# Two transformer layers on one core: the mean of a layernorm as one GpSimd operation per ScalarE tile, and a re-searched instruction order

## The chip, the cores and the metric

One core of a Trainium2 chip. The metric is the device time of the whole program in microseconds (us), the median of several runs. Engines: PE (TensorE matmul, with PEld, its weight loads), DVE (VectorE), ACT (ScalarE), POOL (GpSimd), SP (SyncE, which here issues DMAs).

## The reference

x has 2048 rows of 512 in bfloat16. Four steps run one after the other, each with a residual: A, B, A, B, with the same weights in both layers.

```
x = x + _A_ref(_layernorm(x), A_wqkv, A_w_phi, A_wo)
x = x + _B_ref(_layernorm(x), B_W_gate, B_W_up, B_W_down)
...
phi_q = concat([softmax(q @ w_phi), softmax(-q @ w_phi)]);  phi_k likewise     # 32 heads of 16
kv = phi_k^T v;  z = sum(phi_k);  o = (phi_q kv) / (phi_q z + 1e-6);  A = o @ wo
h = gate * (gate > 0) * up;  B = h @ W_down                                    # F = 1376
```

The attention is linear: kv is one small matrix per head, summed over all 2048 rows. No query can be finished before the last key has been added to kv.

## The kernel before

The rows are 16 tiles of 128 (t = 0 to 15), four to a chunk (c = 0 to 3). A recording layer, `Plan`, notes every operation with its engine; a table of numbers, `ORDER`, then says in which order the operations are written out, and since each engine works its own list in order, that table is the whole schedule. The planner's costs (`TINY`, `X_IN`, the second argument of `pl.op`) steer only the search that once made the table: at build time they have no effect. `BEHIND`, a list of waits that would keep VectorE and GpSimd apart on the port they share, is empty in both kernels.

For each layer and tile:

- **Norm** (class `Norm`). VectorE takes `bn_stats` (line 364) and `bn_aggr` (366); GpSimd adds eps (372) and takes the power -0.5 (374). Tiles are grouped (one or two). A tile is then normalised by the engine that its letter in `STEP["xn1"]` (layer 0) or `STEP["xA"]` (layer 1) names: A is ScalarE (436), D is VectorE and P is GpSimd (448). ScalarE computes scale*x + bias and needs -mean*rstd as its bias; GpSimd makes it in two operations per group, -mean (422) and the product with rstd (424). In layer 1 the chunks c < `STEP["sA"]` take another way (`add_sums`): the residual add on VectorE also gives the sum (542, with an accumulator read), ScalarE gives the sum of squares (388), and six small GpSimd operations follow.
- **Turn**: the normalised tile is transposed, by PE and a copy out of PSUM (457, 259) in the first chunks, by a DMA that SP issues (462, 466) in the others.
- **Keys and values** (`keys_values`): matmul (686), two exponentials on ScalarE (707), values (639, 257), sums over features on VectorE (658, 664, 668; a half may be pre-added by GpSimd, 655), reciprocal (716), and the scale of the features (721), cut between GpSimd and VectorE by a digit of `STEP["ks0"]`. Then PE adds the tile to kv (744): the sums.
- **Queries** (`queries`): matmul (786), exponentials (790), sums, a reciprocal (795), a small product (799, VectorE or GpSimd by `STEP["qq0"]`), a scale (806, by `STEP["qs0"]`), a DMA transpose (808). Queries of the last chunk are held until all sums are done.
- **Attention** (`attention`): after kv is masked into R (766), PE multiplies queries by R (825), VectorE divides (843, 845), the result is turned and projected (876) and added to x (542). Only one PSUM tile of kind q serves 825, so one tile's division must be read out before the next.
- **GLU** (`glu`): gate and up matmuls (589, 569), ScalarE copies (595, 599), VectorE products (602, 606), down (621), residual add (546).

In the names of rows, `sk`, `rk` are the sums and reciprocals of keys, `sq`, `rq` those of queries, `bnst`, `mv` the statistics, `b` any working tile, `ps` and `q` PSUM. Groups of the plan are called k0.5 (keys, layer 0, tile 5), f0.1 (query features), a0.0 (attention) and so on below.

Of the kernel before, what the change touches and what calls it, by code (L numbers as in the profile page):

```python
# [8 lines left out]
P = 128  # L9
# [16 lines left out]
Alu = mybir.AluOpType  # L26
# [3 lines left out]
F32 = mybir.dt.float32  # L30
# [98 lines left out]
WF_IN, WK_IN, WV_IN, WQ_IN, LOADED = 3.57, 5.83, 10.1, 14.03, 13.0  # L129
X_IN = [3.35, 4.26] + [6.46] * 2 + [8.61] * 4 + [11.37] * 4 + [12.62] * 4  # L130
TINY = 0.165
# [197 lines left out]
class Norm:  # L329
# [82 lines left out]
    def normalise(self, n, mv, rstd):  # L412
        st, nc, pl = self.st, self.st.nc, self.st.pl
        tiles, self.tiles, self.mv = self.tiles, [], None
        self.groups.pop(0)
        engs = [self.eng[t % len(self.eng)] for t in tiles]
        nmr = None
        if "A" in engs or self.sums:
            nmr = Buf("ve", [P, 4], F32)
            if not self.sums:  # L420
                self.neg = u = Buf("u", [P, 4], F32)
                pl.op("POOL", TINY, lambda: nc.gpsimd.tensor_scalar_mul(out=u[:, 0:n], in0=mv[:, 0:n, 0], scalar1=-1.0),
                      reads=[(mv, j) for j in range(n)], writes=[(u, 0)])
            pl.op("POOL", TINY, lambda u=self.neg: nc.gpsimd.tensor_tensor(out=nmr[:, 0:n], in0=u[:, 0:n], in1=rstd[:, 0:n], op=Alu.mult),
                  reads=[(self.neg, 0), (rstd, 0)], writes=[(nmr, 0)])
        joint = n == 2 and self.pairs[tiles[0] // 2] == "2" and not any(self.turn and self.turn[t % TPC] != "-" for t in tiles)
        both = Buf("b2", [P, 2, D], BF16) if joint else None
        for j, t in enumerate(tiles):
            ti = t % TPC
            xn = None if joint else Buf("b1", [P, D], BF16)  # L430
            key = (both, j) if joint else (xn, 0)
# [3 lines left out]
            if engs[j] == "A":  # L435
                pl.op("ACT", 0.705, lambda to=to, t=t, j=j: nc.scalar.activation(
                    out=to(), in_=st.X[:, t, :], func=AF.Identity, scale=rstd[:, j:j + 1], bias=nmr[:, j:j + 1]),
                    reads=[("X", t), (rstd, 0), (nmr, 0)], writes=[key])
            else:
# [3 lines left out]
                def scalars(j=j, nmr=nmr):  # L443
# [7 lines left out]
                    reads=[("X", t), (rstd, 0)] + ([(nmr, 0)] if self.sums else [(mv, q) for q in range(n)]), writes=[key], port=not by_pool, long=by_pool)  # L451
# [361 lines left out]
def attention(st, c, pT, norm, L):  # L813
# [72 lines left out]
    "tB0": "A---", "tB1": "---A", "tA": "----", "wev": "ADADAAAADDDAAAAA", "xn1": "APAPDAADPAAPAAAA",  # L886
    "st": "DDDDDDDDDDDDDDDD", "turn": "AAADDAAD", "wake": 20, "fuse0": "AFAA", "fuse1": "FFFF", "gate": 3, "sA": 3,
# [6 lines left out]
}  # L894
ORDER = [int(i) for i in """
# [157 lines left out]
```

## Time and profile before

| | us |
|---|---|
| median of 3 runs (376.4 to 376.66) | 376.47 |
| the profiled execution's own time | 376.54 |
| its span, first to last instruction | 374.8 |
| PE busy | 367.1 |
| DVE busy | 264.1 |
| ACT busy | 210.4 |
| POOL busy | 139.4 |

The granted TensorE clock is 1.00 in every stretch of 10 us. The profile page gives busy shares, the chain of work that ended last, and the costliest groups. A PE that is called busy may be waiting inside a pipelined matmul, but here 512-column matmuls start every 0.215 to 0.216 us over most of the span.

### The profile page before, as it was taken

How to read it: one execution, taken by the hardware profiler on the slowest of the kernel's cores; microseconds unless marked ns; L12 is line 12 of the kernel's file. 1: busy time of each engine (PE TensorE's matmuls, PEld its weight loads, DVE VectorE, ACT ScalarE, POOL GpSimd, SP SyncE). 2: the span in 40 equal slices, each digit the busy share in tenths (PEclk: the TensorE clock that was granted, in tenths of full speed). 3: DMA queues.
4: the chain of work that ended last, by engine and by line, in shares of the span. 5: the costliest groups of instructions: out<-in, count | busy, mean ns of one | idle time of the engine just before them, and what ended most of it. 6: DMA issues, size and time to landing. Idle time of an engine off the chain costs nothing.

```text
span 374.8 us, 6931 instructions
## 1 busy us (share of the span) xinstructions
PE 367.1 (98%) x2530; PEld 195.8 (52%) x2530; DVE 264.1 (70%) x606; ACT 210.4 (56%) x478; POOL 139.4 (37%) x226
## 2 busy tenths in 40 slices
PE   7999989999999999999999999999999999999996
PEld 3454545877645454444444446575546444444453
DVE  6999999997789964486556796898947551244432
ACT  5999987868856525874485184875433334121200
POOL 6999989363140306063522457235200100100000
PEclk9999999999999999999999999999999999999999
DMA  8692694878844407300033045157653501200121
GB/s 259 181 224 46 172 240 90 122 114 156 111 80 91 85 0 115 70 0 2 11 47 71 14 59 100 39 116 127 127 101 71 86 0 31 70 0 16 28 64 63
DMA packets 95746, 31.83 MB, mean 85 GB/s; under 512 B 87424, under 2 KB 95200, under 8 KB 95712
## 3 DMA queue, kind: packets, MB, share of 16 engines
q1 hardware_dynamic: 93024, 27.97, 38.9%
q10 hardware_dynamic: 2688, 3.42, 2.7%
q8 instruction: 20, 0.33, 0.4%
q14 instruction: 14, 0.11, 0.1%
HBM read 8.44 MB, written 2.10 MB: 28 GB/s over the span
## 4 chain that ended last, share of the span: by engine, by line
PE 83%; DVE 8%; POOL 6%; DMA 1%; issue 1%; ACTq 0%
PE ps L589 37%; PE ps L621 20%; PE ps L876 7%; PE ps L786 4%; PE ps L686 4%; PE ps L639 4%; PE ps L569 3%; PE q L825 2%; DVE bnst L364 2%; POOL b L721 1%; PE q L744 1%; DMA X<-in_A_x_dram 1%; DVE b L721 1%; POOL b L655 1%; POOL b L448 1%; DVE rk L716 1%
## 5 line engine op out<-in xcount | busy, mean ns | idle before, releaser
L599 ACT ACTIVATE b<-ps 128x512 bf16<-128x512 f32 (+3 forms) x110 | 50.2, 482 | 61.8 <-PE ps L589 61.1
L589 PE MATMUL ps<-b,wu 128*128 128x512 bf16 (+3 forms) x440 | 81.6, 321 | 0.0
L589 PE MATMUL ps<-b,wg 128*128 128x512 bf16 (+3 forms) x440 | 81.4, 321 | 0.0
L621 PE MATMUL ps<-wd,b 128*128 128x512 bf16 (+4 forms) x374 | 78.7, 366 | 0.0
L621 PEld LDWEIGHTS <-b 128*128 128x128 bf16 (+1 forms) x374 | 35.5, 98 | 39.8
L589 PEld LDWEIGHTS <-wg 128*128 128x128 bf16 x440 | 38.9, 98 | 32.4
L589 PEld LDWEIGHTS <-wu 128*128 128x128 bf16 x440 | 38.5, 98 | 30.0
L602 DVE SCALAR_TENSOR_TENSOR b<-ps,b 128x512 bf16<-128x512 f32 (+2 forms) x60 | 34.1, 594 | 22.0 <-ACT b L599 11.3
L721 POOL TENSOR_TENSOR b<-b,rk 128x1024 bf16<-128x1024 bf16 (+6 forms) x27 | 38.2, 1427 | 24.1 <-DVE rk L716 15.3
L790 ACT ACTIVATE b<-ps 128x512 bf16<-128x512 f32 x64 | 35.8, 618 | 14.3 <-PE ps L786 12.3
L707 ACT ACTIVATE b<-ps 128x512 bf16<-128x512 f32 x64 | 36.4, 637 | 4.2 <-PE ps L686 3.9
L655 POOL TENSOR_TENSOR b<-b 128x256 f32<-128x256 bf16 x39 | 26.7, 701 | 30.8 <-ACT b L790 12.3
L686 PE MATMUL ps<-Wk,b 128*128 128x512 bf16 x128 | 32.4, 379 | 0.0
L876 PE MATMUL ps<-wo,b 128*128 128x512 bf16 x128 | 32.2, 379 | 0.0
L786 PE MATMUL ps<-Wq,b 128*128 128x512 bf16 x128 | 32.2, 379 | 0.0
L639 PE MATMUL ps<-wkv,b 128*128 128x512 bf16 x128 | 31.8, 379 | 0.3 <-ACT b L707 0.3
L546 DVE SCALAR_TENSOR_TENSOR X<-ps,r,X 128x512 bf16<-128x512 f32 (+2 forms) x22 | 14.9, 694 | 22.3 <-PE ps L621 22.3
L542 DVE SCALAR_TENSOR_TENSOR X<-ps,X 128x512 bf16<-128x512 f32 x32 | 21.8, 682 | 8.8 <-PE ps L876 8.4
L595 ACT ACTIVATE b<-ps 128x128 bf16<-128x128 f32 (+2 forms) x50 | 20.8, 431 | 6.5 <-PE ps L589 5.5
L806 POOL TENSOR_TENSOR b<-b,rq 128x512 bf16<-128x512 bf16 x23 | 23.9, 1048 | 0.5
L524 ACT ACTIVATE sq<-b 128x512 bf16<-128x512 bf16 x32 | 20.2, 632 | 6.2 <-DVE b L503 6.0
L845 DVE TENSOR_TENSOR b<-q,dd 128x512 bf16<-128x512 f32 x32 | 21.8, 683 | 0.6
(94 smaller groups left out, 477.1 us busy)
## 6 DMA issues: line engine op xcount, KB each, us to landing
out_dram<-X SPq DMA_DIRECT2D x15, 128.0 KB, 1.9
X<-in_A_x_dram ACTq DMA_DIRECT2D x3, 512.0 KB, 6.4
b<-b SPq DMA_TRANSPOSE x91, 3.1
wd<-in_B_W_down_dram SPq DMA_DIRECT2D x5, 256.0 KB, 3.2
wg<-in_B_W_gate_dram SPq DMA_DIRECT2D x8, 160.0 KB, 3.1
wu<-in_B_W_up_dram SPq DMA_DIRECT2D x8, 160.0 KB, 3.2
wkv<-in_A_wqkv_dram ACTq DMA_DIRECT2D x2, 512.0 KB, 5.6
wq<-in_A_wqkv_dram ACTq DMA_DIRECT2D x1, 512.0 KB, 3.9
```

The source lines that it names most:

```text
L589: nc.tensor.matmul(ps[:], lhsT=wt[:, b, f * P:(f + 1) * P], rhs=xnT[:, lo:hi, b, :], start=(b == 0), stop=(b == NDB - 1))
L599: pl.op("ACT", 0.045 + 0.43 * share, lambda ups=ups, ru=ru, sign=1.0 if fuse else -1.0: nc.scalar.activation(out=ru[:], in_=ups[:], func=A ...
L602: pl.op("DVE", 0.058 + 0.548 * share, dur=0.138 + 0.548 * share, fn=lambda gps=gps, ru=ru, h=h, cs=cs: nc.vector.scalar_tensor_tensor(out= ...
L621: nc.tensor.matmul(yps[:], lhsT=hs[f][:fsz, ti * P:(ti + 1) * P], rhs=st.wd[:fsz, f, cols], start=(f == 0), stop=(f == NFT - 1))
L639: nc.tensor.matmul(vp[:], lhsT=xnT[:, ti, kb, :], rhs=st.wkv[:, kb, D:2 * D], start=(kb == 0), stop=(kb == NDB - 1))
L655: nc.gpsimd.tensor_tensor(out=h[:].rearrange("p j h f -> p j f h"), in0=x[:, :, 0], in1=x[:, :, 1], op=Alu.add)
L686: nc.tensor.matmul(ps[:], lhsT=xnT[:, ti, kb, :], rhs=w(kb), start=(kb == 0), stop=(kb == NDB - 1))
L707: pl.op("ACT", 0.48, lambda s=s, ek=ek, pk=pk: nc.scalar.activation(out=ek[:, :, s, :], in_=pk[:].rearrange("p (j x) -> p j x", j=8), func ...
L721: eng.tensor_tensor(out=phiK[:, lo:hi, :, :].rearrange("p j s (f h) -> p (j s) f h", h=4), in0=ek[:, lo:hi, :, :].rearrange("p j s (f h) - ...
L786: nc.tensor.matmul(pq[:], lhsT=xnT[:, ti, kb, :], rhs=st.Wq2[:, kb, :], start=(kb == 0), stop=(kb == NDB - 1))
L790: pl.op("ACT", 0.48, lambda s=s, eq=eq, pq=pq: nc.scalar.activation(out=eq[:, :, s, :], in_=pq[:].rearrange("p (j x) -> p j x", j=8), func ...
L876: nc.tensor.matmul(yps[:], lhsT=turned(b), rhs=st.wo[:, b, :], start=(b == 0), stop=(b == NDB - 1))
```

## The change

- The bias of a ScalarE tile, -mean*rstd, becomes one GpSimd `tensor_scalar` (mean times rstd times -1, on 128x1) for each tile whose letter is A. The two operations per group (422, 424) go. Where sums are used the old form stays, but `sA` falls from 3 to 0, so that no chunk uses sums: all 12 tiles concerned in layer 1 take `bn_stats` and `bn_aggr` on VectorE, and the ScalarE squares go.
- `xn1`: tiles 3 and 8 are normalised by VectorE, no longer by GpSimd (P to D); tiles 1 and 11 stay with GpSimd.
- `qs0`, `qq0`, `qq1`, `ks1`, `ev1`, `turn`, `xmB1`, `xm1`: single letters move between engines, or join two DMA transposes into one. In layer 0, up to the last sums, one scale more copy out of PSUM and two small products fall to VectorE.
- `ORDER` is new throughout. The planner's constants change with it.

```
-    "st": "DDDDDDDDDDDDDDDD", "turn": "AAADDAAD", "wake": 20, "fuse0": "AFAA", "fuse1": "FFFF", "gate": 3, "sA": 3,
+    "st": "DDDDDDDDDDDDDDDD", "turn": "AADADDDA", "wake": 20, "fuse0": "AFAA", "fuse1": "FFFF", "gate": 3, "sA": 0,
...
-    "tB0": "A---", "tB1": "---A", "tA": "----", "wev": "ADADAAAADDDAAAAA", "xn1": "APAPDAADPAAPAAAA",
+    "tB0": "A---", "tB1": "---A", "tA": "----", "wev": "ADADAAAADDDAAAAA", "xn1": "APADDAADDAAPAAAA",
...
             if not self.sums:
-                self.neg = u = Buf("u", [P, 4], F32)
-                pl.op("POOL", TINY, lambda: nc.gpsimd.tensor_scalar_mul(out=u[:, 0:n], in0=mv[:, 0:n, 0], scalar1=-1.0),
-                      reads=[(mv, j) for j in range(n)], writes=[(u, 0)])
-            pl.op("POOL", TINY, lambda u=self.neg: nc.gpsimd.tensor_tensor(out=nmr[:, 0:n], in0=u[:, 0:n], in1=rstd[:, 0:n], op=Alu.mult),
-                  reads=[(self.neg, 0), (rstd, 0)], writes=[(nmr, 0)])
+                for j in range(n):
+                    if engs[j] == "A":
+                        pl.op("POOL", TINY, lambda j=j: nc.gpsimd.tensor_scalar(
+                            out=nmr[:, j:j + 1], in0=mv[:, j, 0:1], scalar1=rstd[:, j:j + 1], scalar2=-1.0, op0=Alu.mult, op1=Alu.mult),
+                            reads=[(mv, j), (rstd, 0)], writes=[(nmr, j)])
...
-    "qs0": "PPPPPPPPPPDPPDPP", "qs1": "DDPDDPDPPPPPDPDP", "qq0": "PPPPPPPPPPDPPPPP", "qq1": "DDPDPDDDPPPPDPPP",
+    "qs0": "PPPPPPPPPPPPDDPD", "qs1": "DDPDDPDPPPPPDPDP", "qq0": "DPDPPPPPDPDDDDPP", "qq1": "DPPPPPDPDPDPPPPP",
```

In the changed kernel lines after 424 stand three lower on the page: 721 is 724 where the row names the call's line, 655 is 658, 668 is 671, 799 is 802, 806 is 809, 448 is 451.

First place: VectorE at the start, where it makes the first statistics and the copies of transposed weights (`COPY b<-ps`). Before:

```order
L286 TENSOR_TENSOR Wblk<-M_88,wf 128x4x64 x2
L364 BN_STATS bnst_182<-X 128x6
L259 COPY b_156<-ps_157 128x512
L364 BN_STATS bnst_208<-X 128x6
L259 COPY b_186<-ps_187 128x512
L366 BN_AGGR mv_215<-bnst_208 128x2
```

Now:

```order
L286 TENSOR_TENSOR Wblk<-M_88,wf 128x4x64 x2
L259 COPY b_157<-ps_158 128x512
L259 COPY b_165<-ps_166 128x512
L364 BN_STATS bnst_173<-X 128x6
L364 BN_STATS bnst_175<-X 128x6
L366 BN_AGGR mv_177<-bnst_173 128x2
```

Both copies now stand ahead of the statistics of tiles 2 and 3.

Second place: GpSimd at the normalisation of tiles 2 to 7, `ve` being variance plus eps or the bias, `b` the normalised tile. Before:

```order
L372 TENSOR_SCALAR ve_218<-mv_215 128x2
L422 TENSOR_SCALAR u_220<-mv_215 128x2
L374 TENSOR_TENSOR rstd_222<-ve_218,mhalf 128x2
L424 TENSOR_TENSOR ve_224<-u_220,rstd_222 128x2
L448 TENSOR_SCALAR b_313<-X,mv_215,rstd_222 128x512
L372 TENSOR_SCALAR ve_315<-mv_254 128x2
```

Now:

```order
L372 TENSOR_SCALAR ve_257<-mv_177 128x2
L374 TENSOR_TENSOR rstd_259<-ve_257,mhalf 128x2
L423 TENSOR_SCALAR ve_261<-mv_177,rstd_259 128x1
L372 TENSOR_SCALAR ve_306<-mv_283 128x2
L374 TENSOR_TENSOR rstd_308<-ve_306,mhalf 128x2
```

The long row on 128x512 has left GpSimd, and one row of the two for the bias.

Third place: VectorE at the scales of keys 3 to 9, where rows `b<-b,rk` are VectorE's shares of the scale. Before:

```order
L716 RECIPROCAL rk_757<-sk_752 128x64
L795 RECIPROCAL sq_750<-sq_750 128x8x4
L721 TENSOR_TENSOR b_585<-b_584,rk_747 128x896
L721 TENSOR_TENSOR b_501<-b_500,rk_723 128x256
L721 TENSOR_TENSOR b_522<-b_521,rk_734 128x128
L668 TENSOR_REDUCE sq_847<-b_634 128x8x4
L721 TENSOR_TENSOR b_609<-b_608,rk_757 128x512
```

GpSimd's list at that place, before:

```order
L721 TENSOR_TENSOR b_522<-b_521,rk_734 128x896
L721 TENSOR_TENSOR b_501<-b_500,rk_723 128x768
L655 TENSOR_TENSOR b_759<-b_700 128x8x8x4
L799 TENSOR_TENSOR rq_805<-sq_750 128x32
L721 TENSOR_TENSOR b_585<-b_584,rk_747 128x128
L806 TENSOR_TENSOR b_602<-b_602,rq_805 128x8x64
```

VectorE now:

```order
L724 TENSOR_TENSOR b_488<-b_487,rk_715 128x256
L724 TENSOR_TENSOR b_344<-b_343,rk_626 128x128
L724 TENSOR_TENSOR b_574<-b_573,rk_731 128x896
L724 TENSOR_TENSOR b_495<-b_494,rk_628 128x128
L667 TENSOR_REDUCE sq_720<-b_689 128x8x4
L719 RECIPROCAL rk_780<-sk_686 128x64
L802 TENSOR_TENSOR rq_782<-sq_720 128x32
L724 TENSOR_TENSOR b_523<-b_522,rk_780 128x512
```

GpSimd's list there now:

```order
L658 TENSOR_TENSOR b_694<-b_580 128x8x8x4
L724 TENSOR_TENSOR b_488<-b_487,rk_715 128x768
L423 TENSOR_SCALAR ve_552<-mv_416,rstd_543 128x1
L423 TENSOR_SCALAR ve_550<-mv_452,rstd_547 128x1
L809 TENSOR_TENSOR b_580<-b_580,rq_782 128x8x64
```

VectorE's shares now stand in one row of four behind a single long GpSimd scale; the next long GpSimd row (809) needs the small product `rq_782` that VectorE makes after those four.

More of the change, by code (lines that the diff above doesn't have):

```diff
@@ L128 @@
 LATE = ((8, 12), (12, 16), "q")
-WF_IN, WK_IN, WV_IN, WQ_IN, LOADED = 3.57, 5.83, 10.1, 14.03, 13.0
-X_IN = [3.35, 4.26] + [6.46] * 2 + [8.61] * 4 + [11.37] * 4 + [12.62] * 4
-TINY = 0.165
+WF_IN, WK_IN, WV_IN, WQ_IN, LOADED = 3.55, 5.75, 9.75, 14.0, 13.0
+X_IN = [3.35, 4.2] + [6.6] * 2 + [8.25] * 4 + [11.0] * 4 + [12.25] * 4
+TINY = 0.24
 MM, TR, ER, KVM = 0.2155, 0.0555, 0.0318, 0.0318
@@ L420, in normalise @@
             if not self.sums:
-                self.neg = u = Buf("u", [P, 4], F32)
-                pl.op("POOL", TINY, lambda: nc.gpsimd.tensor_scalar_mul(out=u[:, 0:n], in0=mv[:, 0:n, 0], scalar1=-1.0),
-                      reads=[(mv, j) for j in range(n)], writes=[(u, 0)])
-            pl.op("POOL", TINY, lambda u=self.neg: nc.gpsimd.tensor_tensor(out=nmr[:, 0:n], in0=u[:, 0:n], in1=rstd[:, 0:n], op=Alu.mult),
-                  reads=[(self.neg, 0), (rstd, 0)], writes=[(nmr, 0)])
+                for j in range(n):
[3 more added lines that the diff above has]
+                            reads=[(mv, j), (rstd, 0)], writes=[(nmr, j)])
+            else:
+                pl.op("POOL", TINY, lambda u=self.neg: nc.gpsimd.tensor_tensor(out=nmr[:, 0:n], in0=u[:, 0:n], in1=rstd[:, 0:n], op=Alu.mult),
+                      reads=[(self.neg, 0), (rstd, 0)], writes=[(nmr, j) for j in range(n)])
         joint = n == 2 and self.pairs[tiles[0] // 2] == "2" and not any(self.turn and self.turn[t % TPC] != "-" for t in tiles)
@@ L437, in normalise @@
                     out=to(), in_=st.X[:, t, :], func=AF.Identity, scale=rstd[:, j:j + 1], bias=nmr[:, j:j + 1]),
-                    reads=[("X", t), (rstd, 0), (nmr, 0)], writes=[key])
+                    reads=[("X", t), (rstd, 0), (nmr, j)], writes=[key])
             else:
@@ L450, in normalise @@
                     out=to(), in0=st.X[:, t, :], **how, **scalars()),
-                    reads=[("X", t), (rstd, 0)] + ([(nmr, 0)] if self.sums else [(mv, q) for q in range(n)]), writes=[key], port=not by_pool, long=by_pool)
+                    reads=[("X", t), (rstd, 0)] + ([(nmr, j)] if self.sums else [(mv, q) for q in range(n)]), writes=[key], port=not by_pool, long=by_pool)
             if self.turn and self.turn[ti] != "-":
```

149 rows, old and new, of tables (ORDER, STEP) are left out of this document.

## The prediction

> **What bounds the kernel now.** I read the busy shares by stretch first. The columns are the stretch, its length, then busy us (and instructions) of PE, PEld, DVE, ACT, POOL, the clock and DMA.
>
> ```profile
> 0.00:10.00 10.00, 8.01 (x53) 3.84 (x54) 6.76 (x24) 5.54 (x10) 6.44 (x21) 1.00 0.83 268
> 10.00:20.00 10.00, 9.68 (x64) 4.85 (x63) 10.00 (x28) 9.16 (x18) 9.43 (x20) 1.00 0.63 162
> 20.00:30.00 10.00, 9.89 (x75) 5.16 (x74) 9.52 (x21) 10.00 (x22) 9.85 (x14) 1.00 0.81 192
> ...
> 50.00:60.00 10.00, 8.19 (x86) 4.41 (x83) 9.60 (x22) 7.45 (x16) 7.96 (x10) 1.00 0.76 155
> 60.00:70.00 10.00, 9.68 (x126) 7.11 (x125) 9.78 (x28) 9.77 (x27) 8.04 (x13) 1.00 0.81 122
> 70.00:80.00 10.00, 10.00 (x110) 6.81 (x108) 9.54 (x32) 7.09 (x28) 4.59 (x9) 1.00 0.82 134
> 80.00:90.00 10.00, 10.00 (x120) 8.28 (x118) 9.15 (x30) 7.62 (x28) 5.39 (x11) 1.00 0.59 111
> ...
> 140.00:150.00 10.00, 10.00 (x49) 4.55 (x48) 4.72 (x15) 5.37 (x14) 6.36 (x17) 1.00 0.71 107
> ...
> 230.00:240.00 10.00, 9.89 (x126) 5.99 (x125) 7.35 (x16) 4.54 (x10) 3.28 (x4) 1.00 0.14 28
> 240.00:250.00 10.00, 9.91 (x114) 6.60 (x113) 8.89 (x26) 8.74 (x24) 4.62 (x8) 1.00 0.41 80
> 360.00:374.80 14.80, 11.88 (x69) 6.03 (x67) 5.42 (x9) 0.00 (x0) 0.00 (x0) 1.00 0.20 63
> ```
>
> PE is idle for 1.99 us in the first ten, 0.32, 0.11, then 1.81 and 0.32 between 50 and 70, 0.20 around 240, and 2.92 at the end. At 70, 80 and 140 it is full, as in every stretch up to 230; the one from 140 has 49 matmuls in ten us, one every 0.20 us. PE's work is the same in both kernels: the same matmuls and turns, in another order. So the time can fall only by PE's idle time, and can rise by any that is added. Next, who ended PE's idle time:
>
> ```profile
> PE q L744 <- DVE b L721: 1.7, 1, 1.7
> PE ps L277 <- DVE zero L177: 1.2, 1, 1.2
> PE ps L323 <- DVE b L259: 0.5, 1, 0.5
> PE ps L639 <- ACT b L707: 0.3, 1, 0.3
> PE ps L865 <- DVE b L845: 0.3, 1, 0.3
> ```
>
> The start (1.2) stays. The 1.7 us is one wait, for VectorE's scale of keys, ahead of the last sums into kv. The chain of waits (start, length, what) says what made VectorE late:
>
> ```profile
> 29.18 1.87 POOL b L721
> 31.05 1.11 POOL rstd L374
> ...
> 38.12 2.74 DVE b L721 x3
> ...
> 56.72 1.26 PE q L744 x34
> ```
>
> In the twenties and early thirties GpSimd leads, its normalisation's small operations among them, then VectorE up to the sums. Both are full from 10 to 50. After 57 the chain is PE alone but for single steps.
>
> **VectorE's time under GpSimd.** From the order of time of VectorE and, in the fifth row, GpSimd (start, length, engine, line, operation, names, shapes):
>
> ```profile
> 25.72 0.97 DVE L721 TENSOR_TENSOR b<-b,rk 128x256 bf16<-128x256 bf16 x1
> 30.01 2.12 DVE L721 TENSOR_TENSOR b<-b,rk 128x1024 bf16<-128x1024 bf16 x2
> 38.04 2.83 DVE L721 TENSOR_TENSOR b<-b,rk 128x896 bf16<-128x896 bf16 x3
> 41.39 1.25 DVE L721 TENSOR_TENSOR b<-b,rk 128x512 bf16<-128x512 bf16 x1
> 36.59 3.52 POOL L721 TENSOR_TENSOR b<-b,rk 128x896 bf16<-128x896 bf16 x2
> 56.84 0.63 DVE L721 TENSOR_TENSOR b<-b,rk 128x1024 bf16<-128x1024 bf16 x1
> 6.70 0.69 DVE L364 BATCH_NORM_STATS2 bnst<-X 128x6 f32<-128x512 bf16 x1 [0.95 <-DMA X<-in_A_x_dram]
> ```
>
> The scale of 1024 elements takes 0.63 us when GpSimd runs nothing long. By that rate the four other rows need 0.16, 1.18 (1024 and 896), 0.79 (896, 256 and 128) and 0.32, together 2.45. They took 7.17. So **4.7 us** went in waiting for GpSimd: under its two scales from 36.59 to 40.11 alone 2.0.
>
> The Trainium skill ("SBUF — State Buffer", section "SBUF: two separate sides") says that VectorE and GpSimd share a port pair as an exclusive lock for a whole instruction, also against a VectorE operation with two SBUF inputs. The 2.83 us row agrees. The rule speaks against this change, as it makes more VectorE operations of this kind; were each exposed operation to wait as it did on average before, the first rival below would be the result, at its late end.
>
> **The change part by part.** The remaining durations, as groups (count | busy, mean ns):
>
> ```profile
> L448 DVE TENSOR_SCALAR b<-X,mv,rstd 128x512 bf16<-128x512 bf16 x4 | 1.5, 386 | 0.0
> L259 DVE COPY b<-ps 128x512 bf16<-128x512 bf16 x5 | 1.9, 403 | 0.0
> L799 DVE TENSOR_TENSOR rq<-sq 128x32 bf16<-128x32 f32 x8 | 1.5, 187 | 0.1
> L364 DVE BATCH_NORM_STATS2 bnst<-X 128x6 f32<-128x512 bf16 x20 | 13.1, 678 | 1.6 <-DMA X<-in_A_x_dram 1.5
> L366 DVE BATCH_NORM_AGGREGATE mv<-bnst 128x2 f32<-128x6 f32 x20 | 3.0, 165 | 0.1
> L795 DVE RECIPROCAL sq<-sq 128x32 f32<-128x32 f32 x32 | 10.7, 336 | 0.1
> L806 DVE TENSOR_TENSOR b<-b,rq 128x512 bf16<-128x512 bf16 x9 | 3.7, 408 | 0.1
> L448 POOL TENSOR_SCALAR b<-X,mv,rstd 128x512 bf16<-128x512 bf16 x4 | 8.3, 2086 | 0.1
> L422 POOL TENSOR_SCALAR u<-mv 128x2 f32<-128x2 f32 x7 | 1.6, 233 | 0.4
> L424 POOL TENSOR_TENSOR ve<-u,rstd 128x2 f32<-128x2 f32 x13 | 2.7, 207 | 0.5
> L806 POOL TENSOR_TENSOR b<-b,rq 128x512 bf16<-128x512 bf16 x23 | 23.9, 1048 | 0.5
> ```
>
> *GpSimd up to the last sums.* Two normalisations go: -2 x 2.09 = -4.17. Eight operations 422 and eight 424 go, ten of the new form come. The new form is not in the trace; on one element per partition with two scalars it lies between the shorter row, 424 with 0.21 us, and twice 422, 0.47, were its two steps to cost like two operations. I take 0.23, from 422, its nearest row: -8 x 0.233 - 8 x 0.207 + 10 x 0.23 = -1.2. In all -5.4 us (bounds -5.6 and -3.0). The named edit is thus the small part. GpSimd gates nothing but VectorE and the small waits, so this counts through the next item only.
>
> *VectorE up to the last sums.* Two normalisations (2 x 0.386), one copy (0.403) and two products (2 x 0.187) come; one reciprocal (0.336) goes: +1.2. The two copies that now stand ahead of the statistics of tiles 2 and 3 fill the 0.95 us in which VectorE waited for x: -0.6, since they wait for PE's transposes first. And the 4.7 us of waiting: walking both lists of the third place by their durations, GpSimd's scale of tile 5 is the only long one in front of VectorE's four pieces, and its next long row needs the product made after them. I count 0.75 us left, of which 0.5 there; bounds 0 and 5.9 (19 exposed operations in place of 15, at 4.7 / 15 each). Sum: 1.2 - 0.6 - 4.7 + 0.75 = -3.35. The last piece ended at 56.84 + 0.63 = 57.47, and would end at about 54.1.
>
> *PE's wait ahead of the last sums.* PE stood ready at 56.72 - 1.70 = 55.02. VectorE at 54.1 is earlier, so the whole wait goes: **-1.7**. Nothing more than that can come from here: what is late next is PE itself. It would start to come back once VectorE keeps over 0.9 us of waiting beyond my 0.75.
>
> *PE's small waits up to 30 us.* Besides the start 1.99 - 1.2 + 0.32 + 0.11 = 1.2 us. The copies (wait 0.5) now come first and the first value matmuls stand elsewhere, but a wait for a copy of tile 3's turn is new: I take **-0.7**, bounds -1.2 and +0.5.
>
> *R and the first attention tiles* (0.3 us of wait, 865 behind 845). One more sum of query features now stands ahead of the first division, about 0.4 us, and only one q tile exists, so the next matmul 825 queues behind it, with all of PE behind that. **+0.3**, bounds -0.3 and +1.
>
> *Layer 1's norms.* Twelve tiles take statistics on VectorE: 12 x (0.678 + 0.165) = 10.1 us, less twelve accumulator reads. They fall where the down matmuls end, tiles 0 and 1 near 75 and 85, most of them between 100 and 180, where VectorE has room: 4.72 of 10 busy in the stretch from 140. PE's full work from 70 to 230 hides it; without that cover 10 us would be at stake. The rest of the new order, with the waits around 240 (0.20): **+0.2**, bounds -0.2 and +2.
>
> Moved DMA issues: the second copies of weights and tile transposes are issued from SP in another order, some gate weights behind the first query transposes; by the walk they are asked for some 8 us after. Nothing.
>
> **Sum**: -1.7 - 0.7 + 0.3 + 0.2 = -1.9. The profiled execution took 376.54 around a span of 374.8, which would be 374.6 and 372.9. The median, 376.47, is 0.07 below that execution, which is too little to move the number. I predict **374.6 us**. Below 372.9 the small terms would all have to reach their good ends at once: -1.7 - 1.2 - 0.3 - 0.2 = -3.4 makes 373.1.
>
> **Rivals.**
>
> *Nothing gained.* The blocking comes back at its former size, 4.7 us in place of my 0.75: VectorE would end at 54.1 + 3.95 = 58.05, 0.6 later than before, PE's wait would grow by that, and with the other terms, -0.7 + 0.3 + 0.2, the time is 376.5 + 0.6 - 0.2 = **376.9 us**. Its late end, 19 x 0.31 = 5.9 us, gives 1.2 more, 378.1. For it: the program has no wait that keeps the engines apart, so "longer memory" lives in the table alone. Against it: two of GpSimd's 2.09 us operations are gone, and VectorE's pieces now stand together.
>
> *Slower: VectorE falls behind between 60 and 90.* It is busy there for 9.78, 9.54 and 9.15 of 10, that is 1.53 us free of 30. Two tiles' statistics (2 x 0.84), one scale of queries (0.408) and five small products (5 x 0.187) bring 3.0: 1.5 over. If each of these six moved operations is also caught by half of a GpSimd scale of 1.05 (row 806), 3.1 more: 4.6 late. Less the early gain, 1.7 + 0.7 - 0.3 = 2.1, that is +2.5: **379.0 us**. It decides from the point at which VectorE's lateness exceeds the early gain, since PE there lives on projections and GLU products that VectorE hands it. Against it: VectorE enters the stretch over 2 us earlier, and some of its later work is pushed past 90.
>
> **How the numbers follow.** Forecast, 372.9 to 375.7: 0.66. Nothing gained, 375.7 to 377.3: 0.13. Slower, above that: 0.21, of which 0.05 is the late end of the first rival and 0.16 the second. A measurement of this kernel can tell about 0.2%, 0.75 us, from no change. So faster 0.66, within 0.2% 0.13, slower 0.21. The range reaches from 372.8, under the good end of all terms, to 377.6, which takes in the first rival and the near part of the slower cases: about 0.05 lies below and 0.15 above.
>
> **What would show it.** The 1.7 us wait before 744 is gone or under 0.3; the last sums end near 55 to 56, not at 56.72 + 1.26 = 57.98. VectorE's rows 721 (now 724) before that total under 1.5 us more than their 0.63-per-1024 rate. PE is at 10.00 in all stretches from 70 to 230. I am wrong if a new wait on VectorE stands in PE's list between 55 and 100, or if rows of VectorE's scale are still over 1.2 us for 512 elements or fewer.

## The result, and the profile after

The changed kernel takes 374.8 us (median of 20 runs, 374.16 to 376.72) against 376.7 us for the kernel before in the same measurement: a ratio of 0.9948, 95% interval 0.9936 to 0.9960, so 1.9 us or 0.5% faster. The forecast was 374.6 us. The profiled execution took 374.65 us around a span of 372.6 us, 2.2 less than the 374.8 of before. Lines of the code stand three further down than before (721 is now 724, 744 is 747, 825 is 828).

The chain of work that ended last, by engine, shows the change in one row. Before:

```profile
PE 83%; DVE 8%; POOL 6%; DMA 1%; issue 1%; ACTq 0%
```

After:

```profile
PE 95%; DVE 2%; DMA 1%; issue 0%; ACTq 0%
```

GpSimd has left the chain. The list of what ended PE's idle time, after:

```profile
PE ps L277 <- DVE zero L177: 1.2, 1, 1.2
PE ps L310 <- DMA wkv<-in_A_wqkv_dram: 1.0, 1, 1.0
PE q L828 <- DVE b L848: 0.6, 2, 0.4
```

The 1.7 us behind VectorE's scale of keys is gone, and so are the waits of 0.5 (323) and 0.3 (639). New is 1.0 us for the key weights. Of the two waits of 828, the one of 0.4 us ends at 57.76 and stands in the place of the one of 865; the other, 0.2, comes after 230 us, at the first attention tiles of the second layer. The stretches, with the columns as before (PE's busy time is the first number behind the length):

```profile
0.00:10.00 10.00, 7.64 (x54) 3.92 (x55) 6.89 (x24) 4.99 (x9) 6.07 (x19) 1.00 0.82 274
10.00:20.00 10.00, 10.00 (x68) 5.22 (x67) 9.92 (x30) 9.73 (x19) 8.05 (x15) 1.00 0.73 150
20.00:30.00 10.00, 10.00 (x59) 4.96 (x58) 10.00 (x22) 10.00 (x22) 9.74 (x16) 1.00 0.87 215
...
50.00:60.00 10.00, 9.49 (x109) 5.30 (x108) 9.71 (x22) 8.60 (x18) 8.14 (x11) 1.00 0.42 85
60.00:70.00 10.00, 10.00 (x145) 8.11 (x144) 9.67 (x34) 9.08 (x34) 6.25 (x10) 1.00 0.81 147
70.00:80.00 10.00, 9.86 (x114) 6.98 (x112) 9.03 (x30) 6.61 (x24) 4.18 (x6) 1.00 0.77 111
80.00:90.00 10.00, 10.00 (x97) 7.93 (x94) 9.08 (x28) 6.12 (x20) 2.74 (x5) 1.00 0.46 88
...
230.00:240.00 10.00, 9.71 (x108) 5.46 (x105) 7.50 (x18) 6.41 (x13) 2.60 (x4) 1.00 0.27 54
```

PE is idle for 0.51 us from 50 to 70, where it was 2.13. It lost a little at 70 to 80 and 230 to 240, and 0.37 more in the first ten. Now the chain around the last sums (start, length, what):

```profile
53.58 1.53 PE q L747 x48
55.11 0.88 PE ps L789 x4
55.99 0.09 issue
56.08 0.43 PE q L828 x8
56.51 0.02 issue
56.53 0.37 DVE dd L846
56.90 0.02 issue
56.92 0.70 DVE b L848
57.62 0.14 issue
57.76 0.41 PE q L828 x8
```

The last sums end at 55.11 instead of 57.98, and nothing but PE stands ahead of them. What is left is the way from R through the first attention tile and its division back to the one q tile. VectorE's shares of the scale, in order of time:

```profile
33.88 0.93 DVE L724 TENSOR_TENSOR b<-b,rk 128x1024 bf16<-128x1024 bf16 x1
...
37.02 1.34 DVE L724 TENSOR_TENSOR b<-b,rk 128x256 bf16<-128x256 bf16 x4
...
39.19 0.42 DVE L724 TENSOR_TENSOR b<-b,rk 128x512 bf16<-128x512 bf16 x1
...
52.42 1.83 DVE L724 TENSOR_TENSOR b<-b,rk 128x1024 bf16<-128x1024 bf16 x4
```

The four pieces at 37.02 have 256, 128, 896 and 128 elements, 1408 in all. By the rate of 0.63 us for 1024 the first two rows need 0.63 and 0.87 and took 2.27, which is 0.8 us over. Before, the rows of the same kind were 4.7 over. VectorE's last piece ends at 52.42 + 1.83 = 54.25, not at 57.47. I call this excess "lost under GpSimd" below and work it out in the same way for each run.

### The profile page after: what moved, and what is told of

Same layout as the page of the kernel before. It is cut to its first block, busy times and chain, and to the rows that moved or that the text cites. A ratio compares the mean times of both kernels' runs of the same rounds, so it can differ in the third digit from the quotient of the medians.

```text
span 372.6 us, 6861 instructions
## 1 busy us (share of the span) xinstructions
PE 366.3 (98%) x2530; PEld 196.0 (53%) x2530; DVE 269.8 (72%) x626; ACT 201.3 (54%) x452; POOL 128.8 (35%) x192
## 4 chain that ended last, share of the span: by engine, by line
PE 95%; DVE 2%; DMA 1%; issue 0%; ACTq 0%
PE ps L592 37%; PE ps L624 20%; PE ps L642 7%; PE ps L689 7%; PE ps L879 7%; PE ps L789 7%; PE ps L572 3%; PE q L828 2%; PE q L747 2%; DMA wkv<-in_A_wqkv_dram 1%; PE ps L277 1%; PE ps L323 1%; DVE b L848 1%; PE ps L460 0%; DVE X L545 0%; DVE sq L671 0%
## 5 line engine op out<-in xcount | busy, mean ns | idle before, releaser
L624 PE MATMUL ps<-wd,b 128*128 128x512 bf16 (+3 forms) x374 | 79.1, 367 | 0.0
L549 DVE SCALAR_TENSOR_TENSOR X<-ps,r,X 128x512 bf16<-128x512 f32 (+2 forms) x34 | 23.9, 710 | 32.2 <-PE ps L624 32.0
L710 ACT ACTIVATE b<-ps 128x512 bf16<-128x512 f32 x64 | 38.1, 668 | 5.5 <-PE ps L689 5.4
L793 ACT ACTIVATE b<-ps 128x512 bf16<-128x512 f32 x64 | 37.4, 660 | 6.0 <-PE ps L789 6.0
L724 POOL TENSOR_TENSOR b<-b,rk 128x1024 bf16<-128x1024 bf16 (+6 forms) x27 | 37.0, 1384 | 3.4 <-ACT vext L257 2.6
L809 POOL TENSOR_TENSOR b<-b,rq 128x512 bf16<-128x512 bf16 x22 | 23.1, 1053 | 14.2 <-DVE rq L802 13.9
L364 DVE BATCH_NORM_STATS2 bnst<-X 128x6 f32<-128x512 bf16 x32 | 21.4, 684 | 1.0 <-DMA X<-in_A_x_dram 0.6
```

The lines of the kernel that those rows point to most:

```text
L624: nc.tensor.matmul(yps[:], lhsT=hs[f][:fsz, ti * P:(ti + 1) * P], rhs=st.wd[:fsz, f, cols], start=(f == 0), stop=(f == NFT - 1))
L710: pl.op("ACT", 0.48, lambda s=s, ek=ek, pk=pk: nc.scalar.activation(out=ek[:, :, s, :], in_=pk[:].rearrange("p (j x) -> p j x", j=8), func ...
L724: eng.tensor_tensor(out=phiK[:, lo:hi, :, :].rearrange("p j s (f h) -> p (j s) f h", h=4), in0=ek[:, lo:hi, :, :].rearrange("p j s (f h) - ...
L793: pl.op("ACT", 0.48, lambda s=s, eq=eq, pq=pq: nc.scalar.activation(out=eq[:, :, s, :], in_=pq[:].rearrange("p (j x) -> p j x", j=8), func ...
```

## The experiments

Theory 1: VectorE is short of time up to the last sums, and lost 4.7 us of it while GpSimd ran long bf16 operations; the new order and the two normalisations taken off GpSimd end that. Rivals: the named edit of the bias makes the gain; GpSimd's own lead makes it; the order alone makes it. Medians stand beside that of the kernel before from the same set of runs (376.62 for the first four, 376.54 for the next four, 376.61 for the last three). In the profiles of the last seven, 39 of 2,530 matmul records are missing, so that PE's waits are read there and not its busy time.

**The bias alone.** The kernel before, with the new form of the bias:

```diff
-u = -mean                      (GpSimd, per group)
-nmr = u * rstd                 (GpSimd, per group)
+nmr[j] = mean[j] * rstd[j] * -1  (GpSimd, per tile of ScalarE)
```

> The kernel before with the new form of the bias alone: one GpSimd operation for each tile that ScalarE normalises in place of two for each group; order, engines and every other string stay. GpSimd's list gets shorter by some 1.2 us up to the last kv sums, all of it ahead of 33 us, and no long GpSimd operation goes. Theory 1 (the gain comes from VectorE waiting less under GpSimd's long operations, by the new order and the two normalisations that leave GpSimd): the same time within 0.5 us (376.2 to 377.0), TensorE still waits 1.2 to 1.9 us ahead of the last kv sums. Rival (the named edit makes the gain): 374.7 to 375.2, and that wait under 0.5 us.

Measured: 376.44 us, ratio 0.9987 (0.9960 to 1.0014). The wait is still there, and a second one of the same sums:

```profile
PE q L747 <- DVE b L724: 1.7, 1, 1.7
...
PE q L747 <- POOL b L724: 0.4, 1, 0.4
```

Theory 1 holds against this rival; the edit alone can't be told from no change.

**The changed kernel without the bias edit**: the same lines the other way round, at the places of the new ones.

> The changed kernel with the old form of the bias: two GpSimd operations for each group again, put where the new ones stood; order, engines and strings as in the changed kernel. Theory 1: the gain stays, 374.5 to 375.2, no wait of TensorE ahead of the last kv sums. Rival (the named edit makes the gain): back to 376.2 to 377.0, with a wait over 1.2 us there.

Measured: 375.23 us, ratio 0.9942 (0.9921 to 0.9963), just above the upper edge of what theory 1 expected (375.2) and far from the rival. No wait for VectorE is left ahead of the last sums; one of 0.2 us for GpSimd's scale is there. At most some 0.4 us may belong to the edit, and the intervals overlap.

**Three q tiles' pieces later.** The kernel before, VectorE's list near the last sums (f is a q tile's sum or reciprocal):

```diff
-L658 f3, L795 f3, L664 f4, L795 f4      (ahead of the last scales)
 L721 scale of k15
+L664 f4, L795 f4
-L668 f5
 L766 R, L766 R
+L668 f5, L658 f3, L795 f3
```

> The kernel before with nothing but VectorE's order near the last kv sums changed: five pieces for q tiles 3, 4 and 5 (L658 and L795 of tile 3, L664 and L795 of tile 4, L668 of tile 5), 2.6 us of VectorE that the last sums do not need, go behind the last scale piece or behind R, and GpSimd's two powers that read them go with them. GpSimd's long operations and the bias stay. Theory 1 says that the last sums wait for VectorE's last scale piece (57.47): it comes 1.9 us earlier, at 55.5, TensorE's wait of 1.7 us goes to under 0.3, and the time falls by 1.2 to 1.7 to 375.0 to 375.5, if the first q tiles aren't late instead. A rival that puts that wait down to GpSimd's scale pieces (the last ends at 55.03) or to the sums themselves expects the wait to stay at over 1.2 us and 376.5 to 377.

Measured: 377.98 us, ratio 1.0030 (1.0011 to 1.0049): slower, where the theory said 1.2 to 1.7 faster. (The GpSimd operations that went along, called powers above, are the products of 799.) PE's waits:

```profile
PE ps L865 <- DVE b L845: 1.9, 1, 1.9
PE ps L277 <- DVE zero L177: 1.2, 1, 1.2
PE q L744 <- DVE b L721: 1.1, 1, 1.1
```

The wait for the last scale fell from 1.7 only to 1.1: VectorE now had to wait 0.69 us at 50.28 for a half that GpSimd pre-adds (655), which the moved pieces had covered, and a scale piece at 54.46 lost 0.4 under GpSimd. And 1.9 us came up behind the first division, which had to stand behind the pieces that were moved. So VectorE has no time to spare before R or behind it, and moving its work across R gains nothing. Only VectorE time that goes away, work or waiting, counts. Theory 1 was mended in that sense.

**Covering the lock.** The kernel before, again the order alone:

```diff
+L668 f1, L795 f1, L668 k10, L668 f4
 L721 scale of k8, L721 scale of k5, L721 scale of k7
-L668 f1
 L721 scale of k9
-L795 f1 ... L668 k10, L668 f4
```

> The kernel before with four VectorE pieces that read one tile of the pair from PSUM or are copies of scale (L668 and L795 of q tile 1, L668 of k tile 10, L668 of q tile 4; 2.3 us in all) moved ahead of the scale pieces of k tiles 8, 5 and 7, so that they run while GpSimd has its two long scale pieces (36.59 to 40.11), in which the two last of these three lost 1.8 us. No work is added or taken away. Theory 1: VectorE loses 1.0 to 1.8 us less under GpSimd, the last scale piece ends at 55.7 to 56.5, TensorE's wait ahead of the last kv sums falls from 1.7 to under 0.9, and the time is 375.2 to 376.0, if kv sums 5 to 7, which then come 2 us later, find other work of TensorE ahead of them. A rival that sees no price in the sharing between GpSimd and VectorE expects 376.5 to 377.

Measured: 375.49 us in the median, 1.1 below before, with a ratio of 0.9982 (0.9948 to 1.0015), which alone doesn't settle it; the trace does. VectorE's four pieces and GpSimd's two long ones:

```profile
40.43 2.50 DVE L721 TENSOR_TENSOR b<-b,rk 128x896 bf16<-128x896 bf16 x4
```

```profile
36.88 3.14 POOL L721 TENSOR_TENSOR b<-b,rk 128x896 bf16<-128x896 bf16 x2
```

```profile
PE q L744 <- DVE b L721: 0.4, 1, 0.4
```

The sums and the reciprocal that now run beside GpSimd's two scales (3.14 us together) aren't held up; each reads one SBUF tensor, and none reads PSUM as the expectation has it. VectorE's scales start 0.4 us behind the end of GpSimd's. In the trace of before the same four pieces took 2.83 + 1.25 = 4.08; now 2.50. VectorE lost 3.2 us in place of 4.7, and PE's wait fell from 1.7 to 0.4, with no work taken away.

**The two normalisations alone.** The kernel before with

```diff
-"xn1": "APAPDAADPAAPAAAA"
+"xn1": "APADDAADDAAPAAAA"
```

> The kernel before with one string changed: the normalisations of x tiles 3 and 8 go from GpSimd (2.1 us each) to VectorE (about 0.4 us each); order, bias and all else stay. Theory 1, mended by the run with three pieces put later (which showed that VectorE has no time to spare from 31 to about 62 us, so that only VectorE time that goes away counts): GpSimd runs some 4 us ahead, its long pieces meet other pieces of VectorE, and the time follows what VectorE loses under them up to the last kv sums (4.4 us before, 15 operations), plus 0.7 us for the two normalisations: with 2 to 4 us lost, 375.0 to 376.7. A rival says that GpSimd's own lead is the gain (its scale pieces are ready earlier): 374.7 to 375.3 whatever VectorE loses.

Measured: 378.76 us, ratio 1.0048 (1.0029 to 1.0066), slower, and outside both expectations. VectorE's pieces now met other operations, and worse ones:

```profile
29.69 1.82 DVE L721 TENSOR_TENSOR b<-b,rk 128x128 bf16<-128x128 bf16 x1
...
32.56 2.05 DVE L721 TENSOR_TENSOR b<-b,rk 128x1024 bf16<-128x1024 bf16 x1
```

```profile
29.52 1.91 POOL L721 TENSOR_TENSOR b<-b,rk 128x1024 bf16<-128x1024 bf16 x1
```

```profile
PE q L744 <- DVE b L721: 2.0, 1, 2.0
PE ps L457 <- DVE b L448: 1.3, 1, 1.3
```

Counted as before over all such rows, 5.9 us were lost under GpSimd, 1.2 more, though GpSimd had 4.2 us less to do. And a normalised tile that VectorE makes at its old place in the order comes 1.3 us late for its transposes. The rival that puts the gain on GpSimd's lead alone falls.

**The two normalisations back.** The changed kernel with that string the other way round.

> The changed kernel with that string put back: x tiles 3 and 8 are normalised on GpSimd again, 4.2 us of GpSimd's time more and some 0.8 us of VectorE's less; the new order and the new bias stay. Theory 1: the order was found for GpSimd's new load, so that the long pieces come some 4 us later and meet VectorE's scale pieces again, or are late themselves: TensorE waits 1 to 3 us more up to the last kv sums, 375.7 to 377.7. A rival that puts the gain on the order alone expects 374.5 to 375.3.

Measured: 377.18 us, ratio 1.0006 (0.9990 to 1.0022): the whole gain is gone, as the theory's number said, and by the second of the two ways that it named. VectorE lost 1.3 us under GpSimd, only 0.5 more than in the changed kernel. What is late is GpSimd itself, in the twenties:

```profile
PE ps L689 <- ACT b L710: 0.9, 1, 0.9
```

Its normalisation of x tile 11 runs from 21.54 and its scale of k tile 2 from 30.78, in place of 18.01 and 27.17, and PE waits for what follows in several places. The order needs GpSimd's new load, and the new load needs the order: each alone is no faster than before (377.18 and 378.76).

**The statistics of the second layer back.** The changed kernel with

```diff
-"sA": 0
+"sA": 3
```

> The changed kernel with the second layer's row statistics as before: for 12 tiles ScalarE squares and sums (12 times some 0.7 us) and GpSimd has three small operations more for each pair, in place of VectorE's statistics (12 times some 0.83 us); they stand at the places of the operations that they replace, and the sums over rows come with the down projection's addition again. Theory 1 (the step on the second layer's statistics): both ways are hidden behind TensorE's full work from 80 to 230 us, the same time within 0.3 us of the changed kernel (374.5 to 375.1), with no wait of TensorE over 0.3 us there. A rival: VectorE's 10 us more from 80 to 230 cost something (0.5 to 1 us), so that this kernel is at 373.8 to 374.4.

Measured: 375.12 us, ratio 0.9952 (0.9933 to 0.9970). The same as the changed kernel within the intervals. One wait of 0.4 us (592 behind ScalarE's 602) is new between 70 and 230. Where these statistics are made costs nothing that can be measured.

**PE's order around the attention tiles.** The changed kernel, PE's groups at the first of three places (q is a projection, a an attention tile, p its transposes and output projection):

```diff
-q13 a0 q15 a1 p0 q12 p0 p1 a2 q9 p1 p0 q14 a3 g0
+q13 q15 a0 q12 q9 a1 p0 p0 q14 p1 a2 p1 p0 g0 a3 g0
```

> The changed kernel with only the order of some 25 TensorE groups (and of four VectorE pieces) changed, at three places where TensorE still waits: the q projections of tiles 15, 12 and 9 stand around the first attention tile, so that TensorE has work while VectorE divides (0.51 us of waits at 56 to 58); two gate pieces stand ahead of the output projection at 75 (0.3 us); and the q projections of the second layer's tiles are spread between its first attention tiles (0.6 us at 232 to 240). Theory: TensorE's waits that no data forces go, 0.8 to 1.4 us, to 373.3 to 374.1. Rival: VectorE is itself the one that is short there, so that the waits only move, as with the three pieces put later: 374.5 to 375.5.

Measured: 378.30 us, ratio 1.0031 (1.0011 to 1.0051), 3.5 us above the changed kernel. The theory falls, and not only to the rival's value. PE's waits:

```profile
PE ps L879 <- ACT b L257: 1.3, 2, 0.7
PE ps L277 <- DVE zero L177: 1.2, 1, 1.2
PE q L828 <- DVE b L848: 0.8, 1, 0.8
PE ps L592 <- ACT b L257: 0.8, 1, 0.8
PE ps L879 <- DMA b<-b: 0.7, 1, 0.7
```

The q projections that were drawn forward had been what covered ScalarE's copies between transposes and output projection. The wait of 0.4 us around the first attention tiles went, and later ones, longer in all, came: 2.1 us behind ScalarE's copies (879 and 592) between 50 and 80 us. The waits of 828 and of 879 for a DMA, 1.5 together, stand behind 220 us, at the third place; what brought them is not shown. This run shows no work that could be put ahead of the waits around the first attention tiles at no cost.

**One piece put under the lock.** The changed kernel with one VectorE instruction moved:

```diff
-L724 scale of k9           (39.19 to 39.61)
 ...
 L671 k11
+L724 scale of k9
```

> The changed kernel with one VectorE instruction moved: the scale piece of k tile 9 (two inputs in SBUF, 39.19 to 39.61, with no long GpSimd operation beside it) goes five VectorE instructions back, to behind a copy that ends at 44.39, where GpSimd has its long scale piece of k tile 10 (43.73 to 45.63). Kv sum 9, which reads it, comes only at 51.43. Nothing is added; both kernels have the same work on all engines. Theory 1: the piece waits for GpSimd's end, 1.1 to 1.3 us are lost on VectorE, its last scale piece ends at about 55.4 in place of 54.25, kv sum 15 (54.69) waits 0.6 to 0.9 us, and the time rises by as much, to 375.4 to 375.9. A rival to whom the sharing costs nothing expects 374.6 to 375.1 and VectorE's last scale piece at 54.2.

Measured: 375.50 us, ratio 0.9957 (0.9937 to 0.9977); beside it, in the same set, stand 374.85 and 374.86 for two kernels with the changed kernel's order. The piece, GpSimd's operations there, and PE's wait:

```profile
44.04 1.90 DVE L724 TENSOR_TENSOR b<-b,rk 128x512 bf16<-128x512 bf16 x1
...
53.99 1.71 DVE L724 TENSOR_TENSOR b<-b,rk 128x1024 bf16<-128x1024 bf16 x4
```

```profile
43.40 2.27 POOL L724 TENSOR_TENSOR b<-b,rk 128x128 bf16<-128x128 bf16 x2
```

```profile
PE q L747 <- DVE b L724: 0.9, 1, 0.9
```

(Nine instructions lie between the two places, not five.) The piece took 1.90 us in place of 0.42 and ended 0.27 behind GpSimd's 45.67. VectorE's last piece ended at 55.70 in place of 54.25, which is the same 1.5 us, PE waited 0.9, and the time rose by 0.65. The intervals overlap, but the lowest of its runs, 375.22, lies above both of those medians. Theory 1's chain stands link by link.

**The key weights earlier**, two ways, on the changed kernel:

```diff
-LOAD_ACT = ("f", "k", (2, 4), (4, 8), "v")
+LOAD_ACT = ("k", "f", (2, 4), (4, 8), "v")
```

> The changed kernel with two loads swapped in ScalarE's queue: the key half of the weights (512 KB) is issued ahead of the small feature-map weights (16 KB), 0.5 us earlier. Theory on the new wait at 6.22 (the key weights land 0.5 us later in the profile of the changed kernel than in that of before, whose load order is the same, by chance of the DMAs): the weights land 0.3 to 0.5 us earlier, TensorE starts that much earlier on them, and of it 0.2 to 0.5 us reach the end: 374.2 to 374.7. A rival: the first normalised tile is the later one there (its transposes follow at 7.34), so that nothing comes of it, 374.6 to 375.2.

```diff
-LOAD_SP = ((0, 1), (1, 2));  LOAD_ACT = ("f", "k", ...)
+LOAD_SP = ((0, 1), "k");     LOAD_ACT = ("f", (1, 2), ...)
```

> The changed kernel with the key weights issued by SyncE's queue as its second load (at some 1.2 us) and x tile 1 by ScalarE's queue in its place. Theory on the wait at 6.22: what counts is when the 512 KB are issued, and that hardly moves (1.28 to about 1.25), so the time stays within 0.3 us of the changed kernel; x tile 1 lands some 0.5 us later, and VectorE's first statistics with it. A rival: ScalarE's queue is what delays them, and they land 0.5 us earlier, for 374.2 to 374.6.

Measured: 374.85 (ratio 0.9946, 0.9925 to 0.9968) and 374.86 us (0.9944, 0.9921 to 0.9967). In both, PE has the weights at 5.75 to 5.77 and the wait of 1.0 is gone, but the copy of their transposes is awaited instead, in the first:

```profile
PE ps L323 <- DVE b L259: 0.7, 1, 0.7
```

So the new wait of the changed kernel costs nothing that can be measured: the next wait takes its place. No experiment gave a version that beats the changed kernel.

## Why the prediction was right

The main mechanism and the size were right, and by the trace the sum was too small by a little. The busy shares hide part of the waits, since the ends of matmul records are modelled. So I also added up, over all 2,530 matmuls of each kernel, the time from one start to the next beyond what that form takes back to back (0.216 us for 512 columns, less for smaller ones):

```
stretch        before  after
0 to 10          3.19   3.05
10 to 40         1.25   0.41
50 to 60         2.63   0.85
70 to 80         0.00   0.30
230 to 250       0.57   0.73
elsewhere        0.33   0.34
all              7.97   5.68
```

The difference, 2.3, is that of the spans (2.2).

- *PE's wait ahead of the last sums, -1.7*: right. It is gone, and the run with one piece under the lock brings 0.9 of it back by VectorE alone.
- *VectorE up to the last sums, 4.7 to 0.75 us lost, last piece at about 54.1*: right, 0.8 lost and 54.25. That PE itself is what is late next also held: nothing else stands ahead of the last sums now. One part of the way there was wrong. The two copies were to fill 0.6 us of VectorE's wait of 0.95 for x; VectorE now waits 0.73 for the first copy at 6.65, so only 0.2 was won there. About as much as I had counted came instead from two waits that I had not: 0.48 at 22.78 and 0.38 at 36.05 in the trace of before, of which one of 0.21 is left.
- *GpSimd up to the last sums, -5.4*: mis-sized, in the term for the bias. The rows up to 58 us, first before, then after:

```profile
L422 POOL TENSOR_SCALAR u<-mv 128x2 f32<-128x2 f32 (+1 forms) x8 | 1.9, 233 | 0.5
L424 POOL TENSOR_TENSOR ve<-u,rstd 128x2 f32<-128x2 f32 (+1 forms) x8 | 1.8, 224 | 0.2
```

```profile
L423 POOL TENSOR_SCALAR ve<-mv,rstd 128x1 f32<-128x1 f32 x10 | 3.9, 392 | 0.6
```

  Sixteen operations of 3.7 us gave way to ten of 3.9. I had taken 0.23 for one from the nearest row and counted -1.2; it takes about 0.26 undisturbed and up to 0.7 when VectorE holds it up, so that the edit saves GpSimd nothing here. In the kernel before with the new bias alone the same ten took 2.8 us, 0.9 less than the sixteen. In all that is -4.17 + 0.2 = -4.0, inside the bounds. The time doesn't show the miss, because I had called the edit the small part and let GpSimd count through VectorE only. That last step did not hold either: with the two normalisations back GpSimd itself is late, and the kernel loses 2.4 us, while VectorE loses only 0.5 more.
- *PE's small waits up to 30 us, -0.7*: by idle time nothing, 2.36 - 1.2 = 1.16 against 1.2, since 1.0 for the key weights stands where 0.5 for a copy stood. By the table -1.0 up to 40 us, nearly all of it between 10 and 40. The size is inside the bounds, but its place is not the one I named: weights, transposes and copy are one chain, and as the two runs with the weights earlier show, the wait only moves along it.
- *R and the first attention tiles, +0.3*: mis-sized. One wait of 828, 0.4, stands in place of 0.3 (865) and 0.1. PE's idle time from 50 to 70 fell by 1.62, of which the last sums have 1.7, so that about +0.1 is left; the table's -1.8 from 50 to 60 us, again with the last sums, gives no more. The place and the cause, the one q tile behind the division, were right.
- *The second layer's norms and the rest of the order, +0.2*: +0.5 by the table, 0.3 of it at 75 us, at an output projection (879). What it waited for is the DMA that turns its attention tile: issued at 69.81, it landed at 74.84, and the idle time of the weight load ended with it. The chain names VectorE's product of 802 there, which 879 doesn't read. The statistics are not the cause, since putting them back changed nothing.
- *Sum -1.9*: -2.3 by the trace's matmuls, -1.9 by the medians. That it came so close is in part luck, since the misses of the small terms, -0.3, -0.2 and +0.3, go both ways.

Of the signs named beforehand, the wait is gone, the last sums end at 55.11 and the scales are 0.8 us over their rate. PE is not at 10.00 in every stretch from 70 to 230: it has 9.86 from 70 to 80. And by its letter one sign of being wrong came, since a new wait on VectorE stands between 55 and 100: the 0.4 us of 828 at 57.76. It is the wait that the forecast had itself put at +0.3, so that the sign was drawn too wide.

The first rival, that the blocking returns, is real, but not in this order. Both one-sided versions showed what it rests on: with the normalisations alone 5.9 us were lost and the kernel was slower than before. My argument against it, "two of GpSimd's operations are gone", was therefore no reason by itself, although the new order needs it too; that the pieces stand where GpSimd is not was the right one. The second rival didn't come: VectorE is busy for 9.67, 9.03 and 9.08 of ten from 60 to 90, and PE is idle for only 0.14 us there in all.

Open is how much of the gain the bias edit has in the new order: between nothing and 0.4 us, which these intervals don't part. The single letters of the other strings were not run apart from the order, so that their share in it is open as well.

## What to carry to other kernels

Where two engines share a port, what counts is which pairs of operations meet: look for short operations with long durations in the order of time, and let work that is not held up run beside the long ones. Taking load off the engine that blocks can make things worse when the order stays, because the meetings are drawn anew; a change of load and an order made for it have to be judged together. And when an engine is short of time on both sides of a wait, moving its work across the wait only moves the wait.

## What the runs showed of the hardware

- How long a held-up operation takes depends on the other engine and not on its own size: 128 elements per partition took 1.82 us under a scale on GpSimd of 1.91 us, and such a piece took 0.16 in the kernel before, at 28.81, with nothing long on GpSimd.
- It goes the other way, too, for small float operations of GpSimd. The bias took 0.26 us on its own, and of each of these two pairs one met VectorE's pieces (those at 26.28 and 37.02) and took 0.7:

```profile
26.24 0.96 POOL L423 TENSOR_SCALAR ve<-mv,rstd 128x1 f32<-128x1 f32 x2
...
37.39 1.03 POOL L423 TENSOR_SCALAR ve<-mv,rstd 128x1 f32<-128x1 f32 x2
```

- GpSimd's power on 2 elements per partition, which had begun 0.3 us earlier, did not hold up a scale of VectorE's, which took its 0.63 us. A lock held for a whole instruction, as the prediction quotes it, would have done so. In the changed kernel, VectorE and then GpSimd:

```profile
25.28 0.63 DVE L724 TENSOR_TENSOR b<-b,rk 128x1024 bf16<-128x1024 bf16 x1
```

```profile
24.96 0.71 POOL L374 TENSOR_TENSOR rstd<-ve,mhalf 128x2 f32<-128x2 f32 x1
```

- VectorE's sums over rows and reciprocals, which read one tensor, took 0.63 to 0.69 and 0.29 to 0.35 us in the run that covers the lock, under GpSimd's two scales of 3.14 us together, which is what they take elsewhere. The Trainium skill ("SBUF — State Buffer", section "SBUF: two separate sides") names a 2-port performance mode or two SBUF inputs as what brings a VectorE operation into the lock, and the traces agree for two inputs: the scales, which have them, were held up.
- The 512 KB of key weights reached PE between 5.75 and 6.68 us in profiles of kernels that issue them at the same place in the queue, so a wait of up to 1 us there says nothing of an order.
